# Per-step bonus and value copies of a linear-attention front end moved to other engines, with new due dates, in a fused attention, feed-forward and mixture-of-experts kernel

## The chip, the cores and the metric

The kernel runs on one core of one Trainium2 chip. The metric is the device time of one launch in microseconds, the median of several runs. The profiler's span is the time from the first to the last instruction of one profiled execution.

## What is computed

Three parts follow one another. The attention is a linear recurrence with a bonus for the present token (B = 4, H = 8 heads, S = 768, D = 48):

```
for t in range(S):
    kt, vt, rt = (k[:, :, t], v[:, :, t], r[:, :, t])
    cur = np.einsum('bhd,bhe->bhde', u[None] * kt, vt)
    y[:, :, t] = np.einsum('bhd,bhde->bhe', rt, state + cur)
    state = w[None, :, :, None] * state + np.einsum('bhd,bhe->bhde', kt, vt)
```

Its result, 3072 tokens of 384 numbers, goes through a feed-forward network `softplus(x @ w_in) @ w_out` with 2048 inner columns, and that result through eight experts. Tokens are assigned greedily by `x @ w_gate`, each expert takes 384 tokens, and its part is `relu(x @ w1[e]) @ w2[e]`.

The bonus of a token is `v * sum_d(r * k * u)`, one sum per head.

## The kernel before

The attention is done in 24 steps of 128 rows: 64 tokens of each of two batch entries. Three steps make a block of 384 tokens, and the feed-forward network works on eight such blocks. Step n loads k, r and v (`load_step`, lines 360 to 375, two DMAs of 96 KB each, in pieces of 48 numbers) into double buffers KN, RN, VN. It loads v once more in another layout into X, one of three tiles that also hold the recurrent state. In `attention` (line 444), VectorE multiplies k and r by tables of powers of w (ks and rs, lines 453 and 454), TensorE transposes both (lines 466 and 470), and the products of r and k over 64 tokens (line 491) are masked on VectorE (line 499). `fresh` (line 520) and `state` (lines 525 to 537) carry the state to the next X. The bonus is four VectorE operations, lines 541 to 544: r times k, times u (a tile ut with u on all partitions), a reduce over d, and v times the sums. TensorE then multiplies the masked products and the transposed r with X (line 553), and VectorE adds the bonus (line 558, tile xf).

For the first block the result is transposed on TensorE (line 566) and copied to the input of the feed-forward network. Steps 3 to 5, the second block, are transposed there too and split into two halves of 16 bit (lines 578 and 579). From step 6 on, the halves are made first (tile xhl, lines 583 to 585) and turned by a DMA transpose (`turn`, line 569).

Block 0 of the network runs in f32 (first layer at line 673, second at line 785). The later blocks run in three f16 products (lines 678 and 788 to 790). Weights arrive as pairs of 32-bit words, which VectorE puts together with three bit operations (lines 599 to 603) out of four raw buffers ("third<-moe_w_in", "third<-moe_w_out"); 16 such loads make the first layer. While it prepares the second layer, TensorE also transposes w_out (line 633) and multiplies it with the gate (line 637).

All of it up to the last expert is listed as items with an engine or a choice of engines, an assumed duration, dependencies and a due date. `lay_out` (line 148) is a planner that runs at build time. It lets time pass on assumed clocks of all engines and one for DMA, and always issues the ready item of earliest due date on the engine that is free first. The order so found is fixed; each engine then works through its own list and waits on semaphores. The due date of an attention step is `due_att(n)`. A transfer has an assumed `size` in ns of the DMA clock. Where the planner leaves a gap on TensorE it puts in fillers (`keep_warm`, line 143): matmuls on a tile of zeros, into a bank that nobody reads.

Of the kernel before, what the change touches and what calls it, by code (L numbers as in the profile page):

```python
# [21 lines left out]
def tile_kernel(ctx, tc, r, k, v, w, u, w_in, w_out, w_gate, w1, w2, out):  # L22
# [10 lines left out]
    HP = H // 2  # L33
# [216 lines left out]

    T0 = 15500.0
    LEN0 = 43500.0
# [20 lines left out]

    AHEAD = 7500.0

    TURNED, TURN = 6, 1500.0
    HALFL = 4000.0
    HALFL2 = -4000.0
    NLAT = 6
    LATL = 400.0  # L280
    OUTLATE = 5000.0
    RAWL = 17600.0
    BITL = 14000.0
    SPLITL = -3900.0
    WOUTL = 6100.0
    ATT0 = 2600.0
    LOADL = 1600.0

# [18 lines left out]
    XF = several(work, 2, [128, H * D], FT, "xf")  # L307
    XHL = several(work, 2, [128, 2 * DM], HF, "xhl")
    XT2 = several(ffn1p, 2, [128, 2 * KC, BT], HF, "xt")
# [50 lines left out]
    def load_step(n):  # L360
        GROUP[0] = "att"
        b0, s0 = step_tok(n)
        i = n % 2
        due = due_att(n) - LOADL
        for key, src, store in (("kn", k, KN), ("rn", r, RN), ("vn", v, VN)):
            for b in range(2):
                op("sp", 650.0, lambda b=b, src=src, store=store: SP.dma_start(
                    store[i][b * 64:(b + 1) * 64], src[b0 + b, :, s0:s0 + C, :].rearrange("h s d -> s h d")),
                    w=[(key, i, b)], due=due, size=546.0)
        for q in range(2):  # L370
            src = bass.AP(tensor=v.tensor, offset=v.offset + ((b0 * H + q) * S + s0) * D,
                          ap=[[D, C], [2 * S * D, 2 * HP], [1, D]])
            op("sp", 650.0, lambda q=q, src=src: SP.dma_start(
                X[n % 3][(1 - q) * 64:(2 - q) * 64, q].rearrange("p b a d -> p (b a) d"), src),
                w=[("xv", n % 3, q)], due=due + 3.0, size=546.0)

# [13 lines left out]
    op("sp", 1300.0, lambda: [SP.dma_start(wt[q * 64:q * 64 + D], w.rearrange("(p q) d -> q d p", q=2)[q])  # L390
                              for q in range(2)], w=["wt"], due=-1e9, size=168.0)
    op("sp", 450.0, lambda: SP.dma_start(
        ut, bass.AP(tensor=u.tensor, offset=u.offset, ap=[[0, 128], [1, H * D]])), w=["ut"], due=-500.0, size=546.0)
    op("sp", 450.0, lambda: SP.dma_start(gate, w_gate.rearrange("(k p) e -> p k e", p=128)),
# [17 lines left out]
    def powers():  # L412
# [5 lines left out]
        for i in range(6):  # L418
# [3 lines left out]
            DVE.tensor_mul(pw[:, 1, :, C - 2 * m:C - m], pw[:, 1, :, C - m:C], f)  # L422

    op("dve", 3200.0, powers, r=["wt"], w=["pw", ("ar", 1, 0)], due=-1e8)

# [18 lines left out]
    def attention(n):  # L444
# [62 lines left out]
        if n % PC < PC - 1:  # L507
# [27 lines left out]
            for q in range(2):  # L535
                rows = slice(q * 64, (q + 1) * 64)
                op({"act": 413.0, "dve": 470.0}, 0.0, lambda eng, rows=rows, q=q: copied(eng, X[y][rows, q], wx[rows].rearrange("p a b d -> p b a d")),
                   r=[("wx", 0), ("wx", 1)], w=[("st", y, q)], due=due + 3)


        product(rk, RN[i], KN[i], rnk + knk, ["rk"], due + 3)
        product(rk, rk, ut.rearrange("p (h d) -> p h d", h=H), ["ut"], ["rk"], due + 3)
        op("dve", 470.0, lambda: DVE.tensor_reduce(sd, rk, axis=AX.X, op=OP.add), r=["rk"], w=[("sd", i)], due=due + 3)
        product(sv, VN[i], sd[:, :, None].to_broadcast([128, H, D]), vnk + [("sd", i)], [("sv", i)], due + 3)

# [30 lines left out]
        if n < TURNED:  # L576
            op("pe", 321.0, tx, r=[("xf", i), "ident"], w=[(a, g, t) for a in ("xh", "xl", "x2")], due=due + 5, bank=b6)
            op(FROM_PSUM, 0.0, lambda eng: scaled(eng, hi, b6.view(KC, 128), 64.0), w=[("xh", g, t)], due=due + 5, bank=b6)
            op("dve", 470.0, lambda: DVE.scalar_tensor_tensor(lo, b6.view(KC, 128), 64.0, hi, op0=OP.mult, op1=OP.subtract),
               r=[("xh", g, t)], w=[("xl", g, t)], due=due + 5, bank=b6)  # L580
        else:
            xh, xl = XHL[i][:, :DM], XHL[i][:, DM:]
            op(FROM_SBUF, 0.0, lambda eng: scaled(eng, xh, xf, 64.0), r=[("xf", i)], w=[("xhl", i, 0)], due=due + 5)
            op("dve", 470.0, lambda: DVE.scalar_tensor_tensor(xl, xf, 64.0, xh, op0=OP.mult, op1=OP.subtract),
               r=[("xf", i), ("xhl", i, 0)], w=[("xhl", i, 1)], due=due + 5)
            op("sp", 700.0, turn, r=[("xhl", i, 0), ("xhl", i, 1)], w=[("xh", g, t), ("xl", g, t), ("x2", g, t)], due=due + 5, size=TURN)
# [6 lines left out]
    def from_double(src, t, key, due):  # L593
        c = WN[0]
        WN[0] += 1
        raw = RAW[c % 4]
        op("sp", 450.0, lambda: src(raw), w=[("raw", c % 4)], due=due - RAWL, size=1092.0)
        hi, lo = [raw[..., i] if len(t.shape) == 2 else raw[..., i].rearrange("p (k f) -> p k f", k=KC) for i in (1, 0)]
# [22 lines left out]
    def prep_wout(f):  # L621
# [18 lines left out]
        op(FROM_PSUM, 0.0, lambda eng: copied(eng, wT, b1.view(KC, 128)), w=[wt], due=due, bank=b1)  # L640
        op("pe", 330.0, mm, r=[wt, "gate"], due=due, bank=b2)
        op("act", 58.0, lambda: ACT.copy(t[:, DM:], b2.view(E)), w=[("wg", f + 1)], due=due, bank=b2)
# [741 lines left out]
    for p in range(E):  # L1384
# [7 lines left out]
        experts(p)  # L1392
    total = lay_out(items, lambda it: (it.prio, it.n), {}, True)
    s_ps.close()
# [24 lines left out]
```

## Time and profile before

| | us |
|---|---|
| median of 3 runs | 778.96 (777.51 to 786.61) |
| profiled execution, its own time | 775.64 |
| its span | 773.9 |
| TensorE busy (with fillers) | 749.8, 97% |
| VectorE busy | 624.9, 81% |
| ScalarE busy | 404.1, 52% |
| DMA queue q1, share of 16 engines | 38.3% |
| TensorE's share of the chain that ended last | 67% |

Busy time of TensorE counts matmuls from issue to a modelled end, fillers among them, so a busy TensorE may still be waiting for work. Idle time of an engine matters only where another waits for it.

### The profile page before, as it was taken

To read this page: it belongs to the slowest core of one execution; us is meant where nothing else is said; L and a number is where in the kernel's file an instruction comes from. 1 tells how busy PE (TensorE), PEld (TensorE's weight loads), DVE (VectorE), ACT (ScalarE), POOL (GpSimd) and SP (SyncE) were. 2 spreads that over 40 slices of the span, in tenths; PEclk is the share of its full clock that TensorE was granted. 3 is DMA by queue.
4 is the path that set the end of the run, shared out by engine and by line. 5 is a ranking of instruction groups with operands and counts; after the bars stand their busy time and mean duration, and the time that the engine had idled before them with its cause. 6 is when DMAs were issued, how large, how long until landed. Compare 5 with 4: busy or idle time off the path is not lost.

```text
span 773.9 us, 18327 instructions
## 1 busy us (share of the span) xinstructions
PE 749.8 (97%) x7202; PEld 493.0 (64%) x7202; DVE 624.9 (81%) x1711; ACT 404.1 (52%) x808; POOL 81.2 (10%) x109
## 2 busy tenths in 40 slices
PE   7999999999999999999999999999999999998996
PEld 6865677666566666667676666666666665655663
DVE  7898998999998787788999977887789879877420
ACT  2165533799766666567889911211145424436731
POOL 1000000000000000000001000000232131317731
PEclk9999999999999999999999999999999999999999
DMA  7887764412343233333110003441385664837700
GB/s 137 172 183 191 211 171 77 83 22 62 69 91 66 56 68 62 62 67 71 36 22 11 2 12 94 118 121 50 97 208 165 174 175 143 211 108 191 216 31 30
DMA packets 170901, 80.04 MB, mean 103 GB/s; under 512 B 136512, under 2 KB 166464, under 8 KB 170816
## 3 DMA queue, kind: packets, MB, share of 16 engines
q1 hardware_dynamic: 167744, 69.44, 38.3%
q0 software_dynamic: 3072, 9.44, 4.0%
q8 instruction: 56, 0.92, 0.5%
q14 instruction: 29, 0.24, 0.1%
HBM read 61.55 MB, written 9.63 MB: 92 GB/s over the span
## 4 chain that ended last, share of the span: by engine, by line
PE 67%; DVE 18%; issue 4%; ACT 4%; DMA 4%; SPq 1%; POOL 1%; POOLq 0%; ACTq 0%; DVEq 0%
PE bank L678 14%; PE bank L1292 7%; PE bank L788 7%; PE bank L789 6%; PE bank L790 6%; PE bank L785 3%; PE bank L1310 3%; PE bank L1312 3%; PE bank L1311 3%; PE bank L553 2%; PE bank L673 2%; DVE ar L499 2%; DVE gf L691 2%; PE bank L1036 2%; DMA mraw<-moe_w 1%
## 5 line engine op out<-in xcount | busy, mean ns | idle before, releaser
L678 PEld LDWEIGHTS <-wi 128*128 128x128 f16 x1008 | 97.3, 98 | 65.2 <-issue 2.0
L678 PE MATMUL bank<-xt,wi 128*128 128x384 f16 x672 | 127.6, 326 | 0.0
L684 ACT ACTIVATE ta<-bank 128x384 f32<-128x384 f32 x128 | 61.5, 482 | 43.3 <-PE bank L678 30.2
L789 PE MATMUL bank<-wo,g 128*128 128x384 f16 (+1 forms) x240 | 78.4, 327 | 0.9 <-DVE wo L649 0.7
L788 PE MATMUL bank<-wo,g 128*128 128x384 f16 (+1 forms) x240 | 78.5, 327 | 0.0
L790 PE MATMUL bank<-wo,g 128*128 128x384 f16 (+1 forms) x240 | 78.5, 327 | 0.0
L691 DVE SCALAR_TENSOR_TENSOR gf<-bank,ta 128x384 f32<-128x384 f32 x112 | 61.8, 553 | 17.2 <-ACT ta L686 16.0
L678 PE MATMUL bank<-xs,wi 128*128 128x384 f16 x336 | 72.9, 326 | 0.0
L1292 PE MATMUL bank<-g,w1h 128*128 128x384 f16 x384 | 72.9, 326 | 0.0
L685 ACT ACTIVATE ta<-ta 128x384 f32<-128x384 f32 x128 | 66.5, 522 | 2.9
L686 ACT ACTIVATE ta<-ta 128x384 f32<-128x384 f32 x128 | 66.2, 519 | 2.5
L1312 PE MATMUL bank<-w2h,g 128*128 128x384 f16 x192 | 62.6, 326 | 0.0
L1310 PE MATMUL bank<-w2h,g 128*128 128x384 f16 x192 | 62.6, 326 | 0.0
L1311 PE MATMUL bank<-w2l,g 128*128 128x384 f16 x192 | 62.5, 326 | 0.0
L1296 ACT ACTIVATE g<-bank 128x384 f16<-128x384 f32 x64 | 30.7, 489 | 40.4 <-PE bank L1292 24.7
L1292 PEld LDWEIGHTS <-w1h 128*128 128x128 f16 x384 | 35.8, 98 | 22.6 <-issue 0.4
L1299 DVE SCALAR_TENSOR_TENSOR g<-bank,g 128x384 f16<-128x384 f32 x64 | 34.1, 548 | 19.4 <-ACT g L1296 19.3
L698 DVE SCALAR_TENSOR_TENSOR g<-gf,g 128x384 f16<-128x384 f32 x80 | 44.0, 553 | 3.1 <-ACT g L345 1.8
L499 DVE TENSOR_TENSOR ar<-bank,mask 64x256 f32<-64x256 f32 x96 | 40.5, 422 | 4.6 <-PE bank L491 2.3
L345 ACT ACTIVATE x2o<-bank 128x384 f16<-128x384 f32 x19 | 9.3, 490 | 65.3 <-PE bank L790 39.2
L1205 POOL DMA_INDIRECT third<-x2d,idx x24 | 25.8, 1074 | 155.7 <-DVE db L1009 130.0
L1292 PE MATMUL bank<-g,w1l 128*128 128x384 f16 x192 | 41.7, 326 | 0.0
(227 smaller groups left out, 1533.3 us busy)
## 6 DMA issues: line engine op xcount, KB each, us to landing
mraw<-moe_w SPq DMA_DIRECT2D x64, 384.0 KB, 4.0
third<-moe_w_in SPq DMA_DIRECT2D x16, 384.0 KB, 5.0
third<-moe_w_out SPq DMA_DIRECT2D x16, 384.0 KB, 3.5
kn<-k SPq DMA_DIRECT2D x48, 96.0 KB, 3.1
rn<-r SPq DMA_DIRECT2D x48, 96.0 KB, 3.1
vn<-v SPq DMA_DIRECT2D x48, 96.0 KB, 3.0
X<-v SPq DMA_DIRECT2D x48, 96.0 KB, 3.1
x2d<-x2o SPq DMA_DIRECT2D x48, 96.0 KB, 2.2
```

What stands on the lines that cost most here:

```text
L678: PE.matmul(ph, WF[:, f, a, kk, :], x[:, kk, :], start=(i == 0), stop=(i == 3 * KC - 1))
L684: op("act", 371.0, lambda: ACT.activation(ta, bank.view(BT), AF.Abs), w=[("ta", c)], due=due, bank=bank)
L685: op("act", 413.0, lambda: ACT.activation(ta, ta, AF.Exp, scale=-1.0), w=[("ta", c)], due=due)
L686: op("act", 413.0, lambda: ACT.activation(ta, ta, AF.Ln, bias=1.0), w=[("ta", c)], due=due)
L691: op("dve", 470.0, lambda: DVE.scalar_tensor_tensor(gf, bank.view(BT), 0.0, ta, op0=OP.max, op1=OP.add), r=[("ta", c)], w=[("gf", c)], due ...
L788: PE.matmul(p, gh[:, f, ts], WU[:, f, 0, :no], start=(f == 0), stop=False)
L789: PE.matmul(p, gh[:, f, ts], WU[:, f, 1, :no], start=False, stop=False)
L790: PE.matmul(p, gl[:, f, ts], WU[:, f, 0, :no], start=False, stop=(f == FC - 1))
L1292: PE.matmul(ph, a[:, kk, fs], XH[p][:, x0 + kk, :], start=(i == 0), stop=(i == 3 * KC - 1))
L1310: PE.matmul(po, h1h[:, f, js], w2h[:, fz, :], start=(f == 0), stop=False)
L1311: PE.matmul(po, h1h[:, f, js], w2l[:, fz, :], start=False, stop=False)
L1312: PE.matmul(po, h1l[:, f, js], w2h[:, fz, :], start=False, stop=(f == FB - 1))
```

## The change

The first six steps get the bonus on TensorE. The transposed r (in its PSUM bank) and the transposed k, both with their powers of w, which leave one factor w in the product of a token with itself, are multiplied on VectorE into rkT. rkT lies in the buffers of xhl. Four f32 matmuls per step (`sums`), with rkT as the weight and a table uw of two columns (u times w of one head each), give the sums in PSUM, and VectorE multiplies v by them from there. The ut tile is needed only from step 6 on and is loaded later; u comes a second time, transposed, as uq. For the same steps X gets v by four copies from VN on ScalarE or VectorE, as the planner chooses, and the two DMAs are left out. TURNED goes from 6 to 3, so steps 3 to 5 are turned by DMA. Due dates and several assumed costs are new, the planner's clocks of SP and VectorE start at 1000 and 900 ns, and so every engine's order is new.

```diff
-    T0 = 15500.0
+    T0 = 16250.0
...
-    AHEAD = 7500.0
-
-    TURNED, TURN = 6, 1500.0
-    HALFL = 4000.0
-    HALFL2 = -4000.0
+    AHEAD = 10500.0
+
+    TURNED, TURN = 3, 1500.0
+    SUMMED = 6
+    COPIED = 6
+    HALFL = 9000.0
+    HALFL2 = -1500.0
...
-    OUTLATE = 5000.0
+    OUTLATE = 8750.0
...
-    BITL = 14000.0
+    BITL = 16000.0
...
-    ATT0 = 2600.0
-    LOADL = 1600.0
+    ATT0 = 850.0
+    LOADL = 2400.0
...
-    XHL = several(work, 2, [128, 2 * DM], HF, "xhl")
+    XHL2 = work.tile([128, 2, 2 * DM], HF, name="xhl")
+    XHL = [XHL2[:, i] for i in range(2)]
...
-                    w=[(key, i, b)], due=due, size=546.0)
+                    w=[(key, i, b)], due=due, size=640.0)
+        if n < COPIED:
+            for q in range(2):
+                for b in range(2):
+                    op({"act": 260.0, "dve": 180.0}, 0.0, lambda eng, q=q, b=b: copied(
+                        eng, X[n % 3][(1 - q) * 64:(2 - q) * 64, q, b],
+                        VN[i][b * 64:(b + 1) * 64].rearrange("p (a q) d -> p a q d", q=2)[:, :, q, :]),
+                        r=[("vn", i, b)], w=[("xv", n % 3, q)], due=due_att(n) + 2.5)
+            return
...
+    op("sp", 1300.0, lambda: [SP.dma_start(uq[q * 64:q * 64 + D], u.rearrange("(p q) d -> q d p", q=2)[q])
+                              for q in range(2)], w=["uq"], due=-1000.0, size=168.0)
     op("sp", 450.0, lambda: SP.dma_start(
-        ut, bass.AP(tensor=u.tensor, offset=u.offset, ap=[[0, 128], [1, H * D]])), w=["ut"], due=-500.0, size=546.0)
+        ut, bass.AP(tensor=u.tensor, offset=u.offset, ap=[[0, 128], [1, H * D]])), w=["ut"], due=due_att(3), size=1200.0)
...
+    uw = const.tile([128, HP, 2], FT, name="uw")
+    uq = const.tile([128, HP], FT, name="uq")
+    rkT = XHL2.rearrange("p a m -> p (a m)").bitcast(FT)[:, :HP * 128].rearrange("p (a t) -> p a t", a=HP)
+
+    def factors():
+        DVE.memset(uw, 0.0)
+        for q in range(2):
+            DVE.tensor_mul(uw[q * 64:q * 64 + D, :, q], uq[q * 64:q * 64 + D], wt[q * 64:q * 64 + D])
+
+    op("dve", 300.0, factors, r=["wt", "uq"], w=["uw"], due=2.5)
...
+        if n < SUMMED:
+            op("dve", 602.0, lambda: DVE.tensor_tensor(rkT, b2.view(HP, 128), kT, op=OP.mult), r=[("kT", i)], w=["rkT"] + [("xhl", a, b) for a in range(2) for b in range(2)],
+               due=due + 3, bank=b2)
+
+            def sums():
+                for pr in range(HP):
+                    PE.matmul(b7.view(H)[:, 2 * pr:2 * pr + 2], rkT[:, pr, :], uw[:, pr, :], start=True, stop=True)
+
+            b7 = Bank("att")
+            op("pe", 900.0, sums, r=["rkT", "uw"], w=[("sd", i)], due=due + 3, bank=b7)
+            op("dve", 470.0, lambda: DVE.tensor_tensor(sv, VN[i], b7.view(H)[:, :, None].to_broadcast([128, H, D]), op=OP.mult),
+               r=vnk, w=[("sv", i)], due=due + 3, bank=b7)
+        else:
+            bonus()
...
-        op("sp", 450.0, lambda: src(raw), w=[("raw", c % 4)], due=due - RAWL, size=1092.0)
+        op("sp", 450.0, lambda: src(raw), w=[("raw", c % 4)], due=due - RAWL, size=1900.0)
...
-        op("pe", 330.0, mm, r=[wt, "gate"], due=due, bank=b2)
+        op("pe", 670.0, mm, r=[wt, "gate"], due=due, bank=b2)
...
-    total = lay_out(items, lambda it: (it.prio, it.n), {}, True)
+    total = lay_out(items, lambda it: (it.prio, it.n), {"sp": 1000.0, "dve": 900.0}, True)
```

`bonus()` holds the four operations of lines 541 to 544. The order of the loads on SP at the very start, before (kn, rn, vn with numbers 93, 91, 95 are the buffers of even steps, 94, 92, 96 those of odd ones):

```order
L390 DMA wt<-w 48x4x1 x2
L607 DMA third<-moe_w_in 128x3x256
L367 DMA kn_93<-k 64x8x48 x2
L367 DMA rn_91<-r 64x8x48 x2
L367 DMA vn_95<-v 64x8x48 x2
L373 DMA X_97<-v 64x8x48 x2
L392 DMA ut<-u 128x384
L607 DMA third<-moe_w_in 128x3x256
L367 DMA kn_94<-k 64x8x48 x2
```

and now:

```order
L401 DMA wt<-w 48x4x1 x2
L370 DMA kn_93<-k 64x8x48 x2
L370 DMA rn_91<-r 64x8x48 x2
L370 DMA vn_95<-v 64x8x48 x2
L370 DMA kn_94<-k 64x8x48 x2
L370 DMA rn_92<-r 64x8x48 x2
L370 DMA vn_96<-v 64x8x48 x2
L647 DMA third<-moe_w_in 128x3x256
L403 DMA uq<-u 48x4x1 x2
```

The loads of the second step stand in fifth to seventh place, ahead of the first weight third; the X loads and ut are gone from this stretch.

VectorE in the third step (number 2, the even buffers), up to its result xf_114, before:

```order
L599 TENSOR_SCALAR wi<-third 128x384
L340 TENSOR_TENSOR rk_104<-rk_104,ut 128x384
L353 COPY ar_111<-bank_85 64x8x64
L527 TENSOR_TENSOR wx_113<-bank_86,wx_113 128x4x48
L527 TENSOR_TENSOR wx_113<-bank_81,wx_113 128x4x48
L543 TENSOR_REDUCE sd_105<-rk_104 128x8
L499 TENSOR_TENSOR ar_111<-bank_80,mask 64x4x64 x2
L499 TENSOR_TENSOR ar_111<-bank_82,mask 64x4x64 x2
L340 TENSOR_TENSOR wx_113<-wx_113,sq 128x384
L340 TENSOR_TENSOR sv_107<-vn_95,sd_105 128x384
L353 COPY X_97<-wx_113 64x384
L558 TENSOR_TENSOR xf_114<-bank_83,sv_107 128x384
```

and now, from the copy into ar_111 on:

```order
L356 COPY ar_111<-bank_85 64x8x64
L572 TENSOR_TENSOR xhl<-bank_85,kT_109 128x512
L641 SCALAR_TENSOR_TENSOR wi<-third,wi 128x384
L356 COPY X_99<-vn_95 64x192
L523 TENSOR_TENSOR ar_111<-bank_80,mask 64x4x64 x2
L356 COPY X_99<-vn_95 64x192
L523 TENSOR_TENSOR ar_111<-bank_81,mask 64x4x64 x2
L551 TENSOR_TENSOR wx_113<-bank_86,wx_113 128x4x48
L551 TENSOR_TENSOR wx_113<-bank_84,wx_113 128x4x48
L581 TENSOR_TENSOR sv_107<-vn_95,bank_83 128x384
L343 TENSOR_TENSOR wx_113<-wx_113,sq 128x384
L598 TENSOR_TENSOR xf_114<-bank_82,sv_107 128x384
```

The product with ut (line 340 into rk) and the reduce are replaced by one product into xhl's buffer (rkT, line 572), v is multiplied by a PSUM bank (line 581), and two of the value copies into X_99 stand between the masks.

TensorE around the sixteenth and last chunk of block 0's first layer, before (lines 466 and 470 belong to step 5, lines 633 and 637 prepare the second layer, line 785 is the second layer):

```order
L637 MATMUL bank_86<-gate,third 128x8 x3
L637 MATMUL bank_81<-gate,third 128x8 x3
L466 MATMUL bank_85<-identf,ks_103 128x128 x4
L673 MATMUL bank_86<-xt_118,wi 128x384 x3
L470 MATMUL bank_81<-identf,rs_101 128x128 x4
L633 MATMUL bank_85<-identf,wo 128x128 x3
L785 MATMUL bank_83<-wo,g_128 128x392 x2
```

and now (line 713 is the chunk, line 593 is step 6's product with X, line 577 the sums of step 5; lines 673 and 143 are the first preparation of the second layer and fillers):

```order
L593 MATMUL bank_82<-X_97,ar_111 64x48 x16
L577 MATMUL bank_84<-uw,xhl 128x2 x4
L713 MATMUL bank_81<-xt_117,wi 128x384 x3
L673 MATMUL bank_83<-identf,wo 128x128 x3
L143 LDWEIGHTS still
L143 MATMUL bank_87<-still 128x128
```

Steps 3 to 6 have now been through their product with X ahead of that chunk, where before it was steps 3 and 4, with step 5 begun; the preparation of the second layer starts behind it instead of ahead.

## Rows read from the trace of the kernel before

**Rows 1.** Windows: busy us (x instructions) by engine, then granted clock, DMA share, GB/s

```profile
0.00:39.00 39.00, 32.73 (x588) 29.13 (x588) 31.81 (x88) 8.82 (x15) 2.53 (x12) 0.96 0.76 154
39.00:86.00 47.00, 44.75 (x355) 28.87 (x356) 43.97 (x104) 26.65 (x56) 0.00 (x0) 1.00 0.78 193
86.00:142.00 56.00, 56.00 (x698) 40.91 (x697) 51.05 (x119) 22.92 (x57) 0.00 (x0) 1.00 0.60 138
142.00:774.00 632.00, 616.26 (x5565) 394.04 (x5563) 498.09 (x1404) 345.72 (x682) 78.72 (x97) 1.00 0.37 91
```

**Rows 2.** Groups by line, 0 to 40 us: the fillers; busy us, mean ns

```profile
L143 PE MATMUL bank<-still 128*128 128x128 bf16 x258 | 19.2, 233 | 1.0 <-DVE wt L389 1.0
```

**Rows 3.** Timeline, 0 to 38 us: start us, us, engine, line; in brackets the wait

```profile
16.59 0.56 DVE L340 TENSOR_TENSOR ks<-kn,pwn 128x384 f32<-128x384 f32 x1 [1.26 <-DMA kn<-k]
...
17.29 0.94 PE L466 MATMUL bank<-identf,ks 128*128 128x128 f32 x4 [1.51 <-DVE ks L340]
...
37.27 0.56 DVE L558 TENSOR_TENSOR xf<-bank,sv 128x384 f32<-128x384 f32 x1
...
37.88 0.55 PE L566 MATMUL bank<-identf,xf 128*128 128x128 f32 x3
```

**Rows 4.** Timeline of TensorE, 39 to 83 us

```profile
39.00 4.14 PE L673 MATMUL bank<-xt,wi 128*128 128x384 f32 x12
...
49.56 1.14 PE L553 MATMUL bank<-X,ar 128*64 128x48 f32 x32
...
52.67 0.49 PE L566 MATMUL bank<-identf,xf 128*128 128x128 f32 x3
...
62.46 0.66 PE L466 MATMUL bank<-identf,ks 128*128 128x128 f32 x4 [1.56 <-DVE ks L340]
...
81.36 1.50 PE L637 MATMUL bank<-gate,third 128*128 128x8 f32 x12
...
82.72 0.63 PE L466 MATMUL bank<-identf,ks 128*128 128x128 f32 x4
```

**Rows 5.** Window on VectorE, from the first ks to the third result

```profile
9.17:37.83 28.66, 23.08 (x53) 0.94 0.83 170
```

**Rows 6.** Groups of VectorE, 9.17 to 37.83 us: busy us, mean ns, idle before

```profile
L499 DVE TENSOR_TENSOR ar<-bank,mask 64x256 f32<-64x256 f32 x12 | 5.1, 422 | 0.4
...
L353 DVE COPY ar<-bank 64x512 f32<-64x512 f32 x3 | 2.1, 694 | 0.9 <-ACT ar L351 0.9
...
L340 DVE TENSOR_TENSOR rk<-rk,ut 128x384 f32<-128x384 f32 x3 | 1.7, 552 | 1.8 <-DMA ut<-u 1.8
...
L543 DVE TENSOR_REDUCE sd<-rk 128x8 f32<-128x384 f32 x3 | 1.6, 549 | 0.0
...
L527 DVE TENSOR_TENSOR wx<-bank,wx 128x192 f32<-128x192 f32 x4 | 1.2, 352 | 0.7 <-PE bank L520 0.7
...
L340 DVE TENSOR_TENSOR rk<-rn,kn 128x384 f32<-128x384 f32 x2 | 1.1, 548 | 0.0
...
L353 DVE COPY X<-wx 64x384 f32<-64x384 f32 x3 | 1.1, 356 | 0.1
```

**Rows 7.** Timeline of SP's issues, 6 to 10 us

```profile
6.60 1.31 SPq L373 DMA_DIRECT2D X<-v  x2
...
7.96 0.62 SPq L392 DMA_DIRECT2D ut<-u  x1
...
9.10 1.29 SPq L367 DMA_DIRECT2D kn<-k  x2
```

**Rows 8.** Timeline of VectorE: the late third, and the last first-layer weight

```profile
59.70 0.36 DVE L599 TENSOR_SCALAR wi<-third 128x384 int32<-128x384 int32 x1 [2.38 <-DMA third<-moe_w_in]
...
80.54 0.55 DVE L603 SCALAR_TENSOR_TENSOR wi<-third,wi 128x384 int32<-128x384 int32 x1
```

**Rows 9.** Windows of 1 us: busy us, TensorE's granted clock after POOL

```profile
16.00:17.00 1.00, 0.00 (x0) 0.00 (x0) 0.41 (x1) 0.00 (x0) 0.00 (x0) 1.00 0.36 64
18.00:19.00 1.00, 1.00 (x12) 0.97 (x10) 0.91 (x4) 0.59 (x1) 0.00 (x0) 0.50 1.12 184
```

More of the change, by code (lines that the diff above doesn't have):

```diff
@@ L374, in load_step @@
                 X[n % 3][(1 - q) * 64:(2 - q) * 64, q].rearrange("p b a d -> p (b a) d"), src),
-                w=[("xv", n % 3, q)], due=due + 3.0, size=546.0)
+                w=[("xv", n % 3, q)], due=due + 3.0, size=640.0)
     wt = const.tile([128, HP], FT, name="wt")
@@ L538, in attention, with bonus @@
                    r=[("wx", 0), ("wx", 1)], w=[("st", y, q)], due=due + 3)
[L541 to L544, printed above, removed]
+        def bonus():
+            product(rk, RN[i], KN[i], rnk + knk, ["rk"], due + 3)
+            product(rk, rk, ut.rearrange("p (h d) -> p h d", h=H), ["ut"], ["rk"], due + 3)
+            op("dve", 470.0, lambda: DVE.tensor_reduce(sd, rk, axis=AX.X, op=OP.add), r=["rk"], w=[("sd", i)], due=due + 3)
+            product(sv, VN[i], sd[:, :, None].to_broadcast([128, H, D]), vnk + [("sd", i)], [("sv", i)], due + 3)
+        if n < SUMMED:
[10 more added lines that the diff above has]
+            bonus()
         b5, b6 = Bank("att"), Bank("att")
@@ L582, in attention @@
             xh, xl = XHL[i][:, :DM], XHL[i][:, DM:]
-            op(FROM_SBUF, 0.0, lambda eng: scaled(eng, xh, xf, 64.0), r=[("xf", i)], w=[("xhl", i, 0)], due=due + 5)
+            op(FROM_SBUF, 0.0, lambda eng: scaled(eng, xh, xf, 64.0), r=[("xf", i)], w=[("xhl", i, 0), "rkT"], due=due + 5)
             op("dve", 470.0, lambda: DVE.scalar_tensor_tensor(xl, xf, 64.0, xh, op0=OP.mult, op1=OP.subtract),
```

## The prediction

> **What bounds the kernel now.** I read the stretches first. From 86 us to 142 us TensorE is busy 56.00 of 56.00 us and after that 616 of 632, so nearly all of the program is a queue of matmuls; what can be had lies ahead of 86 us. Before 39 us TensorE looks busy too (32.73 us), but the groups of the first 40 us show 258 fillers, matmuls on a zero tile that only keep the engine active, with 19.2 us of it [rows 1, 2]. They run where TensorE would wait. So I read the timeline of the first 39 us for what it waits for: the first matmul of the first feed-forward layer (line 673) starts at 39.00, right behind the ScalarE copy of the third step's transposed result, whose addition on VectorE (line 558) starts at 37.27 [rows 3, 4]. Three attention steps must be through before it, and they are a chain on VectorE: from the first ks product at 9.17 to the end of that addition at 37.83 VectorE works 23.08 of 28.66 us [rows 5]. The largest waits in it are two transfers: ut (1.8 us ahead of the product at line 542, as the group shows) and kn of the second step, 1.26 us ahead of 16.59 [rows 3, 6]. That kn is issued only at 9.10, because SP has put a weight third, the X copy of v and ut ahead of it, at 0.65 us an issue [rows 7].
>
> From 39 to 86 us TensorE (44.75 of 47) and VectorE (43.97 of 47) are both near full [rows 1]. TensorE's longest wait there, 1.56 us at 62.46, is for a ks product that stood behind a weight third that landed late (VectorE 2.38 us idle before 59.70) [rows 4, 8].
>
> **The change part by part.** *The way to the first layer.* In the new order on SP, kn, rn and vn of both first steps are the first twelve loads, and X and ut no longer stand between them; at the same 0.65 us an issue kn of the second step is issued at about 6 to 7.3 us instead of 9.10 to 10.4, with one weight third and the X pair less in the queue. Its ks product can start at about 11 instead of 16.59, and ut is not needed by the first six steps. I take both waits as gone: -3.1 us.
>
> VectorE's own list over these three steps: leaving are three products with ut (1.7 us), three reduces (1.6), two of the three r·k products (1.1; the first stood before 9.17) [rows 6]; the halving at line 347 (0.35, as the like operation at 59.70) and two of three state copies into X (2 x 0.36) go to ScalarE, which is busy 8.8 us of the first 39, or stand after the addition now. That is 5.5 us. Coming are three products of the transposed r and k (128x512 from PSUM). No row has this shape; between the 0.55 of a 128x384 operation and the 0.69 of the 64x512 PSUM copy I take 0.69, whose free size is the same: 2.1. Further the table uw (a fill and two products of 48x4; 0.4, hardly more than one such copy), three value copies left on VectorE (64x192; under the 0.36 of 64x384, I take 0.25: 0.75) and two more weight-preparing instructions (0.35 and 0.5) [rows 6, 8]. Sum 4.1, so the list is 1.35 us shorter.
>
> What is added in waits: the first value copy stands ahead of ks(0) on VectorE and, on ScalarE, two of them stand between the two copies of the power table; all wait for vn(0), which SP issues by about 6 us as its third pair. With ks(0) at 9.3 instead of 9.17 and rs(0) about 0.5 later than now, that hides behind the second ks. Behind the table uw on VectorE stand a weight third and the second step's state; uq, needed by it, is issued around 11 us and could take as long as kn did (issued by 10.4, used at 16.59), up to 1 us late. The sums on TensorE (four matmuls, two passes each) delay the next step's transpose on an engine full of fillers. So 28.66 - 3.1 - 1.35 = 24.2 us from 9.3, the addition ends at 33.5, and the first layer starts 1.17 us behind it as now (37.83 to 39.00): 34.7. **Term 1: -4.3 us.** If a part of the other 2.5 us idle goes too and the products take 0.55: -6.2; if uw comes late and the new hand-overs cost 1.5: -1.8.
>
> *TensorE's own work after that.* The sums of steps 3 to 5 lie in the full stretch. The nearest row is the gate product, 128x8 in f32 on a 128x128 weight: 12 records advance TensorE by 1.36 us (81.36 to 82.72), 0.113 each [rows 4]. Eight records a step are 0.92, three steps 2.8; bounds 1.6 (a narrower moving operand at 60% of it) and 3.2. Turning the results of the second block by DMA removes three transposes; the one at 52.67 takes 0.49 us with its latency, of which I take 0.35 as TensorE's own [rows 4]: -1.0. **Term 2: +1.8** (+0.1 to +2.2). For these steps ScalarE reads SBUF instead of PSUM and the transfer lands long before block 1 begins; its cover is the whole first layer. On SP a turn stands behind its step's VectorE work with two weight thirds behind it, but four third buffers are already issued ahead, so I cost it at nothing; without that cover it would cost what the late third at 59.70 cost.
>
> *The first layer, 39 to 86 us.* With X gone from the queue the 2.38 us wait of VectorE for a third, and with it TensorE's 1.56 us, should go. Against this the new due dates pull 1.5 attention steps ahead of the last first-layer chunk, and VectorE has to serve them. One step with the new sum is about 6.9 us there (ks, rs, state product, result addition and value product 0.5 to 0.55 each, masks 1.7, the two copies 0.69 and 0.36, states 0.7, the new product 0.69) [rows 3, 6], so 10.3 more; the two common steps save 1.5; weight preparation of the second layer moves behind (2.4), the split of the turned results and its copy drop 0.8; five more activation sums and half a preparation come (2.8): +8.4. The last first-layer weight, ready at 81.0 now [rows 8], would be ready at 81.0 - 4.3 + 8.4 - 2.4 = 82.7 and its chunk through at about 85, where it ends at 85.1 today. At that point TensorE will have done two more steps (six groups of small matmuls each, from 0.5 to the 1.1 of line 553 at 49.56: 3.2), less a begun one (0.9) and less second-layer preparation (2.2, by the 1.50 of its longest group): 3.3 us more useful work. So this path gives -3.5 in all, and I set **term 3: -1.0** (-2.7, that wait and as much again in small ones; +3, if VectorE is late again).
>
> **Sum:** -4.3 + 1.8 - 1.0 = -3.5 us against the profiled execution's 775.64 (its span 773.9 and 1.7 around it): 772.1. The runs' median, 778.96, lies 3.3 above that execution; a median of the changed kernel should stand alike: 775.4, a ratio of 0.995.
>
> **The clock.** With fillers taken away TensorE could fall to the lower clock. Now it has no work from 16 to 17 us, and from 18 to 19 the granted clock is 0.50, which is 1.2 of 2.4 GHz; the transposes at 17.29 take 0.94 us instead of the 0.66 they take at 62.46 [rows 3, 4, 9]. The Trainium skill (TensorE: Matmul & The Clock Gate, section "The HAM clock gate") says the low clock is the state to which an idle array falls back and activity is what releases it, and the trace agrees. By that rule the new order, with 188 fillers ahead of the first layer for 258, would pay once more if one of its gaps is as long as the one before 17.29; the sum itself keeps the clock as it is, since the gap that caused the fall (kn) goes.
>
> **The rivals.**
> *A, more than the sum.* VectorE, relieved by 0.75 us a step, keeps up, the late third and the small waits of 39 to 86 us all go, and the first layer starts at 33: -6.2 + 1.0 - 2 = -7, 772. For it: the DMA relief, twelve transfers of 96 KB less. Against: VectorE has more to do before the sixteenth chunk.
> *B, slower.* VectorE becomes the bound of the first layer. The 1.5 steps pulled ahead put 10.3 us on it in a stretch where it is already busy 43.97 of 47; if it waits there as much as today (3 us) and the hand-overs to TensorE and ScalarE cost 4 more, the last weight comes at 90, TensorE ends the layer at 92 with 3.3 us more done: 92 - 85.1 - 3.3 = +3.6, median 782.6. It decides from about 86 us for the last weight on. For it: both engines near full in one stretch; against: the count above, which has it at 82.7.
> *C, the change does not reach the end.* The start is earlier but the sums on TensorE and filler gaps behind the first layer eat it: -1.8 + 2.2 - 0.4 = 0, 779.
>
> **How the numbers follow.** Forecast (772.5 to 778) 0.50; A 0.22; C 0.15; B 0.13. The forecast's own bounds are -1.8 + 2.2 and -6.2 + 0.1 - 2.7 on the terms; the range 766 to 783 takes A's far end (-9.5 with the two runs' scatter of 3) and B. 2% is 15.6 us, about what a measurement of this kernel can tell from no change; only a start that gets nearly half of the fillers' time and the stalls back at once (763) would be faster by that, 0.04, and B would have to be four times as bad, 0.03; within 0.93.
>
> **What would show it.** Right: first matmul of the first layer at 34 to 36; second ks at about 11; no ut wait; no half clock before 25; the sums about 0.9 us a step; last first-layer weight at 82 to 84; TensorE full from 90 on with the same tail. Wrong: the first layer later than 37 (then uq, vn or the sums are in the chain, term 1), the last weight after 86 (B), a sum of over 1.2 us, or a changed stretch behind 142 us, which I took as it is.

## The result, and the profile after

The changed kernel takes 773.17 us (median of 20 runs, 770.23 to 775.0), the kernel before 780.16 in 20 runs beside it (775.66 to 786.61): a ratio of 0.9904, 95% interval 0.9885 to 0.9924. It is 1% faster, and the interval excludes 1. The forecast was 775.4 and 0.995: the sign and the range held, and the gain was about twice what was worked out. The profiled execution of the changed kernel took 770.23, with a span of 768.4 (773.9 before): 5.5 us less, where the sum said 3.5. The record has the mean granted clock of every run: 0.996 on average in these 20 runs, and 0.992 in the 82 runs of the kernel before that stand beside the experiments below. 0.004 of 775 us is 3.1 us, so by estimate some three of the seven us between the medians are less time at the low clock.

Windows of the changed kernel, with the columns of [rows 1]; the cuts at 33.40 (where the first layer starts), 86 and 142 us:

```profile
0.00:33.40 33.40, 30.68 (x541) 27.42 (x541) 29.04 (x84) 12.25 (x26) 2.53 (x12) 1.00 0.75 152
33.40:86.00 52.60, 51.17 (x565) 34.77 (x564) 50.89 (x118) 35.92 (x77) 0.00 (x0) 1.00 0.81 182
86.00:142.00 56.00, 55.37 (x513) 38.10 (x513) 54.06 (x124) 21.86 (x55) 0.00 (x0) 1.00 0.72 151
142.00:767.00 625.00, 613.01 (x5565) 392.48 (x5564) 486.87 (x1388) 337.47 (x669) 78.33 (x97) 1.00 0.36 90
```

The stretch ahead of the first layer is 5.6 us shorter than the 39.00 of [rows 1]. In the second stretch TensorE idles 1.43 us (2.25 before) and VectorE 1.71 (3.03 before): both are fuller than they were.

The timeline of the changed kernel: SP's issue of kn of the second step, the first three ks products, the table uw, the third step's addition, and the first layer ([rows 3, 4, 7] before):

```profile
6.12 1.31 SPq L370 DMA_DIRECT2D kn<-k  x2
8.55 0.56 DVE L343 TENSOR_TENSOR ks<-kn,pwn 128x384 f32<-128x384 f32 x1
10.13 0.55 DVE L343 TENSOR_TENSOR ks<-kn,pwn 128x384 f32<-128x384 f32 x1
...
15.93 0.07 DVE L443 MEMSET uw<- 128x8 f32 x1
16.03 0.35 DVE L445 TENSOR_TENSOR uw<-uq,wt 48x4 f32<-48x4 f32 x2
...
23.59 0.55 DVE L343 TENSOR_TENSOR ks<-kn,pwn 128x384 f32<-128x384 f32 x1
...
31.69 0.55 DVE L598 TENSOR_TENSOR xf<-bank,sv 128x384 f32<-128x384 f32 x1
32.30 0.55 PE L606 MATMUL bank<-identf,xf 128*128 128x128 f32 x3
33.41 4.14 PE L713 MATMUL bank<-xt,wi 128*128 128x384 f32 x12
```

kn is issued 3 us earlier than in [rows 7] and the second ks comes at 10.13 for 16.59. No bracket stands behind the two products with uq at 16.03, so VectorE does not wait for uq here.

The groups of the changed kernel in its first 40 us (fillers, and the new operations with the ones beside them) and the one wait of VectorE between 33 and 86 us:

```profile
L143 PE MATMUL bank<-still 128*128 128x128 bf16 x189 | 15.0, 238 | 1.0 <-DVE wt L400 1.0
L354 ACT COPY X<-vn 64x192 f32<-64x192 f32 x13 | 4.5, 350 | 1.2 <-DMA vn<-v 1.0
L577 PE MATMUL bank<-uw,xhl 128*128 128x2 f32 x24 | 3.2, 254 | 0.2 <-DVE xhl L572 0.2
L572 DVE TENSOR_TENSOR xhl<-bank,kT 128x512 f32<-128x512 f32 x3 | 2.1, 689 | 0.0
L581 DVE TENSOR_TENSOR sv<-vn,bank 128x384 f32<-128x384 f32 x3 | 1.7, 552 | 0.0
L356 DVE COPY X<-vn 64x192 f32<-64x192 f32 x4 | 1.0, 256 | 0.1
```
```profile
DVE ar L356 <- ACT ar L354: 0.7, 1, 0.7
```

The 2.38 us wait for a weight third of [rows 8] is gone, and TensorE's wait for ks with it; TensorE's longest wait there is now 1.0 us. The new 128x512 product takes 0.69 us and the 64x192 copy 0.26, as taken (0.69 and 0.25).

Further on, TensorE and the last first-layer weight on VectorE ([rows 4, 8] before):

```profile
41.84 1.05 PE L577 MATMUL bank<-uw,xhl 128*128 128x2 f32 x8
42.75 0.57 PE L713 MATMUL bank<-xt,wi 128*128 128x384 f32 x1
...
78.80 0.56 DVE L643 SCALAR_TENSOR_TENSOR wi<-third,wi 128x384 int32<-128x384 int32 x1
...
82.29 2.18 PE L713 MATMUL bank<-xt,wi 128*128 128x384 f32 x6
```

Eight records of a step's sums advance TensorE by 42.75 - 41.84 = 0.91 us (0.92 taken). The last weight is ready at 79.4, where 82.7 was expected.

**An account for TensorE.** From the first matmul of the first layer on, TensorE is full, so I split its time up to the last matmul of the f16 first layers (446.3 us before, 440.8 after) into idle time, fillers and the rest, its own work. The window with all instructions and the one with the fillers alone, first of the kernel before, then of the changed one:

```profile
39.00:446.30 407.30, 402.79 (x4324) 266.73 (x4325) 362.54 (x864) 283.05 (x609) 2.95 (x11) 1.00 0.37 80
39.00:446.30 407.30, 11.50 (x60) 5.62 (x60) 1.00 0.37 80
```
```profile
33.40:440.80 407.40, 404.54 (x4349) 268.25 (x4349) 361.23 (x866) 283.33 (x615) 2.73 (x11) 1.00 0.39 81
33.40:440.80 407.40, 10.97 (x69) 6.03 (x68) 1.00 0.39 81
```

The first number behind the length is the busy time: idle is 407.30 - 402.79 = 4.51 before and 2.86 after, fillers 11.50 and 10.97, own work 391.3 and 393.6. So the end, that last matmul, moved by -5.6 (start) - 1.65 (idle) - 0.53 (fillers) + 2.3 (own work) = -5.5 us, and from there on both kernels take 327.6 us. The same split of every run (us, one profiled execution each; "low clock" is the part of the own work lost at a granted clock under 1, from windows of 1 us; "behind" is the rest of the span, from the end to the last instruction). The last column is an estimate over all runs that the ratio uses: from the time of each, (1 - mean granted clock) x span is taken off, and the median of what is left is set against that of the kernel before beside it:

| | start | idle | fillers | own work | low clock in it | end | behind | median | ratio and interval | less low clock |
|---|---|---|---|---|---|---|---|---|---|---|
| before | 39.0 | 4.5 | 11.5 | 391.3 | 0 | 446.3 | 327.6 | | 1 | 0 |
| after | 33.4 | 2.9 | 11.0 | 393.6 | 0 | 440.8 | 327.6 | 773.17 | 0.9904 [0.9885, 0.9924] |  |
| e12_after | 33.4 | 2.9 | 11.0 | 395.2 | 1.7 | 442.4 | 329.8 | 773.09 | 0.9923 [0.9895, 0.9952] | -4.1 |
| e1_dates | 40.8 | 2.7 | 10.2 | 393.4 | 0 | 447.1 | 330.9 | 779.38 | 1.0016 [0.9993, 1.0039] | +3.6 |
| e2_parts | 35.0 | 5.2 | 10.4 | 397.7 | 5.1 | 448.3 | 329.5 | 777.05 | 0.9971 [0.9939, 1.0002] | -1.4 |
| e7_warm | 36.7 | 6.1 | 11.5 | 391.5 | 0 | 445.8 | 329.5 | 777.47 | 0.9976 [0.9946, 1.0006] | -0.3 |
| e8_loads | 36.2 | 5.8 | 14.2 | 393.2 | 1.7 | 449.4 | 325.9 | 777.9 | 0.9985 [0.9959, 1.001] | +0.6 |
| e11_copies_old | 36.4 | 4.4 | 11.5 | 391.3 | 0 | 443.6 | 335.4 | 777.27 | 0.9969 [0.9937, 1.0002] | -1.0 |
| e3_nosums | 35.0 | 1.6 | 11.9 | 391.2 | 0 | 439.7 | 330.6 | 770.51 | 0.9858 [0.981, 0.9906] | -6.5 |
| e5_noturn | 33.4 | 1.5 | 8.8 | 394.6 | 0 | 438.2 | 328.7 | 769.59 | 0.9858 [0.9808, 0.9907] | -6.4 |
| e6_sums2 | 33.5 | 2.1 | 11.0 | 395.5 | 0 | 442.1 | 329.5 | 776.51 | 0.9938 [0.9904, 0.9971] | -2.7 |
| e4_nocopies | 35.2 | 3.2 | 18.6 | 392.9 | 0 | 450.0 | 330.3 | 781.49 | 1.0014 [0.9979, 1.0049] | +4.8 |
| e9_nocopies_free | 35.9 | 1.5 | 12.0 | 392.5 | 0 | 441.8 | 332.2 | 774.36 | 0.9916 [0.9879, 0.9954] | -3.3 |
| e10_copies | 35.0 | 2.4 | 15.3 | 392.1 | 0 | 444.8 | 328.6 | 776.66 | 0.9985 [0.9955, 1.0014] | 0.0 |

The ends lie nearly in the order of the ratios. e2_parts and e8_loads, which lost clock in their profiled execution, end later than their ratios would have it. The experiments are read by these columns, with three cautions.

First, the clock. The 82 runs of the kernel before lie between 773.41 us (mean clock 0.998) and 790.21 (0.986). A line through them falls by 8.7 us for each 0.01 of clock, near the 7.8 that 1% of the span is, and more than half of their variance goes with it. In its profiled execution the kernel before lost 1.7 us ahead of its first layer ([rows 9]), which the account holds in the start. With the low clock taken off both, the ends differ from that of the kernel before by -3.8 (after), -3.9 (e12_after), -1.4 (e2_parts), -1.0 (e11_copies_old), -2.5 (e6_sums2) and -6.4 (e5_noturn), close to the last column. The others agree with it within 1.6, but e8_loads, which is 2.5 off.

Second, behind the end the profiled executions spread from 325.9 to 335.4 us, and the account does not cover that part: the profiled execution of e11_copies_old ends its span 5.1 us later than that of the kernel before, although its end is 2.7 earlier.

Third, one execution differs from the next. Up to its fillers e7_warm is the kernel before, yet it is 1.0 us earlier there (below). So differences of under 1 us in a term are not firm.

### The profile page after: what moved, and what is told of

Read it like the earlier page. It is cut to its first block, busy times and chain, and to the rows that moved or that the text cites. A ratio compares the mean times of both kernels' runs of the same rounds, so it can differ in the third digit from the quotient of the medians.

```text
span 768.4 us, 18301 instructions
## 1 busy us (share of the span) xinstructions
PE 750.2 (98%) x7179; PEld 492.8 (64%) x7179; DVE 620.9 (81%) x1710; ACT 407.5 (53%) x824; POOL 80.9 (11%) x109
## 4 chain that ended last, share of the span: by engine, by line
PE 65%; DVE 15%; issue 9%; DMA 3%; ACT 3%; POOL 2%; SPq 1%; POOLq 0%; DVEq 0%
PE bank L718 18%; PE bank L828 7%; PE bank L830 7%; PE bank L829 7%; PE bank L1332 5%; PE bank L593 3%; PE bank L825 2%; PE bank L1350 2%; PE bank L1352 2%; PE bank L1351 2%; PE bank L1076 1%; POOL out L1360 1%; PE bank L515 1%; DVE ar L523 1%; PE bank L713 1%
```

## The experiments

The theory was that the first layer starts earlier, that this reaches the end, and that the sums cost TensorE their own time. Its main rival was that an early start is eaten by the first layer, so that other parts or the dates bring the gain. In e7_warm, e6_sums2 and e12_after the order of every engine stays; after each of the other edits the planner lays it out anew, so what such a run shows is the price of a move together with that of an order.

**Dates alone, moves alone.** e1_dates is the changed kernel with all three moves undone:

```diff
-    TURNED, TURN = 3, 1500.0
-    SUMMED = 6
-    COPIED = 6
+    TURNED, TURN = 6, 1500.0
+    SUMMED = 0
+    COPIED = 0
...
-        ut, ...), w=["ut"], due=due_att(3), size=1200.0)
+        ut, ...), w=["ut"], due=-500.0, size=546.0)
```

> The changed kernel with all its due dates, assumed costs and clock starts, but none of the three moves: bonus on VectorE, v for X by DMA, steps 3 to 5 turned on TensorE; ut is loaded early again. If the moves bring the time (start theory): the X loads and ut stand in SP's queue again, the first matmul of the first layer starts at 37 to 40 us, and the total is within 3 us of the kernel before (ratio 0.996 to 1.004). If the new due dates bring it by themselves: first layer at about 35, ratio 0.990 to 0.993.

Measured: 1.0016; the first layer starts at 40.8. The dates alone bring nothing; with the low clock taken off they cost 3.6 us, by estimate. (The load of uq and the table uw, of no use here, are still in, and VectorE waits 0.80 us for uq.)

e2_parts has the three moves with the dates, costs and clock starts of before (ut's own date and cost, which go with the sums, stay new):

```diff
-    T0 = 16250.0
+    T0 = 15500.0
...
-    AHEAD = 10500.0
+    AHEAD = 7500.0
...
-    total = lay_out(items, lambda it: (it.prio, it.n), {"sp": 1000.0, "dve": 900.0}, True)
+    total = lay_out(items, lambda it: (it.prio, it.n), {}, True)
```

> The three moves with the old due dates, assumed costs and clock starts. Start theory: X and ut are out of the queue, so kn of step 1 is issued at about 7.5 to 9 us in place of 9.1 to 10.4 (a weight third still stands ahead of it), the first layer starts at 35 to 36.5, total 3 to 4 us under the kernel before (ratio 0.995 to 0.996). If the due dates bring it all: ratio 0.999 to 1.001.

Measured: 0.9971, and an interval that holds 1. The start is 4.0 us earlier, but the layer lasts to 91. Windows of this kernel, and the chunk of six matmuls that lies in them:

```profile
82.00:84.00 2.00, 1.84 (x15) 1.75 (x15) 1.89 (x7) 1.59 (x4) 0.00 (x0) 0.87 0.42 166
84.00:86.00 2.00, 2.00 (x31) 1.74 (x31) 1.89 (x4) 0.91 (x2) 0.00 (x0) 0.50 0.03 8
...
92.00:94.00 2.00, 2.00 (x8) 1.58 (x7) 2.00 (x6) 1.85 (x5) 0.00 (x0) 0.57 0.96 165
```
```profile
87.77 4.19 PE L713 MATMUL bank<-xt,wi 128*128 128x384 f32 x6
```

The granted clock is 0.50 (1.2 of 2.4 GHz) from 84 to 93 us, and six matmuls take 4.19 us that take 2.18 in the changed kernel at 82.29. That is 5.1 of the 448.3; without it the end would lie 3.1 us ahead of that of the kernel before, by estimate. The other nine runs bear it out: the four with a mean clock of 0.990 to 0.992 take 777.4 to 779.7 us, the three with 0.997 or more take 771.9 to 773.3, where the two runs of the kernel before at 0.997 beside them take 774.2 and 776.3. So the moves alone are worth something, by estimate 1.4 us, and the clock hides it.

**The start alone.** e7_warm is the kernel before with 26 fillers ahead of the second step's ks transposes, where TensorE fell to half clock in [rows 9]:

```diff
         def tk():
+            for _ in range(26 if n == 1 else 0):
+                PE.matmul(banks[7][:, :128], still, still, start=True, stop=True)
             for pr in range(HP):
```

> The kernel before with 26 more filler matmuls ahead of the transposes of step 1's ks, where TensorE waits 1.5 us for that product; nothing else moves. If the clock matters: the granted clock stays at 1.00 from 15 to 21 us, the chain behind it gets 0.5 to 1 us shorter, the runs scatter less than those of the kernel before, ratio 0.997 to 0.999. If the clock at that place costs nothing on the way to the first layer: ratio 1.000, same scatter.

Measured: 0.9976, interval holding 1. The same two windows as [rows 9], then VectorE between them and the first layer, in the kernel before:

```profile
16.00:17.00 1.00, 1.00 (x17) 0.99 (x15) 0.94 (x3) 0.00 (x0) 0.00 (x0) 1.00 0.63 106
18.00:19.00 1.00, 1.00 (x51) 0.94 (x44) 1.00 (x2) 0.00 (x0) 0.00 (x0) 1.00 0.93 270
```
```profile
20.67 0.62 DVE L527 TENSOR_TENSOR wx<-bank,wx 128x192 f32<-128x192 f32 x2 [0.65 <-PE bank L520]
...
23.01 0.69 DVE L353 COPY ar<-bank 64x512 f32<-64x512 f32 x1 [0.62 <-ACT ar L351]
```

and in e7_warm, with the late third and TensorE's longest wait from 33 to 90 us (us in total, times, longest):

```profile
15.60 0.56 DVE L340 TENSOR_TENSOR ks<-kn,pwn 128x384 f32<-128x384 f32 x1 [0.83 <-DMA kn<-k]
...
19.06 0.62 DVE L529 TENSOR_TENSOR wx<-bank,wx 128x192 f32<-128x192 f32 x2
...
20.70 0.69 DVE L353 COPY ar<-bank 64x512 f32<-64x512 f32 x1
...
34.95 0.56 DVE L560 TENSOR_TENSOR xf<-bank,sv 128x384 f32<-128x384 f32 x1
...
58.75 0.36 DVE L601 TENSOR_SCALAR wi<-third 128x384 int32<-128x384 int32 x1 [3.74 <-DMA third<-moe_w_in]
```
```profile
PE bank L468 <- DVE ks L340: 2.9, 1, 2.9
```

The clock holds and the first layer starts 2.3 us earlier. Not all of that is the clock. The second ks is already 1.0 us earlier (15.60 for the 16.59 of [rows 3]), because ut and kn landed earlier in this execution; kn is issued at 9.1 us in both kernels, and the fillers run from 15.05 on. From that ks to the third step's addition it takes 19.35 us for 20.68, and the two waits of 0.65 and 0.62 are gone: the half clock cost about 1.3 us at the start, by one execution of each kernel.

But the late third is used only 0.95 us earlier than in [rows 8] (58.75 for 59.70), VectorE now waits 3.7 us for it and TensorE 2.9 (2.38 and 1.56 before, [rows 4, 8]), and the end moves by 0.5. Here the main rival is right: the first layer eats most of the earlier start, and the lower median goes with the higher clock (-0.3 us without it).

e8_loads is the kernel before with the loads of the second step put ahead of the X loads and ut:

```diff
-        due = due_att(n) - LOADL
+        due = due_att(n) - LOADL if n != 1 else -1598.0
...
-        ut, ...), w=["ut"], due=-500.0, size=546.0)
+        ut, ...), w=["ut"], due=-500.0 + 1500.0, size=546.0)
```

> The kernel before, with only step 1's loads of k, r and v moved ahead of the X loads, and ut behind the second weight third, in SP's queue; the planner orders all else anew. Start theory: the wait for kn (1.3 us) goes, the one for ut may move, second ks at 11 to 13 us in place of 16.6, first layer at 36.5 to 38, total 1 to 2.5 us under the kernel before (0.997 to 0.999). If the three moves of the bonus and copies are needed to shorten VectorE's chain: first layer at 38.5 to 39, ratio 1.000.

Measured: 0.9985. The start is 2.8 us earlier, but VectorE waits 5.6 us for one third, idle grows by 1.3, fillers by 2.7, and 1.7 us go to the low clock:

```profile
DVE wi L599 <- DMA third<-moe_w_in: 5.6, 1, 5.6
```

e11_copies_old is the kernel before with the value copies alone (e2_parts with SUMMED = 0, TURNED = 6 and ut loaded early again):

> The kernel before with the value copies alone, with the old dates, planner costs and clock starts. Theory that copies and dates are needed together: 0.995 to 1.000, span 773 to 776, the first layer starting 2 to 4 us earlier than 39 us and ending no earlier than 84. Rival, that the copies alone bring the gain: as the run of copies with new dates, 0.980 to 0.990, span 764 to 769.

Measured: 0.9969. The start is 2.6 us earlier, idle, fillers and own work are those of before, and the end moves by 2.7. With the X loads gone the early start does carry through: VectorE's wait for a third is down to 1.1 us here:

```profile
DVE wi L639 <- DMA third<-moe_w_in: 1.1, 1, 1.1
```

The ratio agrees (0.31% is 2.4 us), though the interval just holds 1. Part of this is the clock: the granted clock is 1.00 up to the first layer here, and with the low clock taken off both kernels 1.0 us is left.

**One move taken back.** e3_nosums has the bonus on VectorE again (and ut loaded early), e5_noturn the transposes of steps 3 to 5 on TensorE, e4_nocopies the X loads:

```diff
-    SUMMED = 6
+    SUMMED = 0
```


> The changed kernel with the bonus back on VectorE in the first six steps and ut loaded early; value copies, turns and dates as changed. If the bonus move carries part of the gain: VectorE's list to the first layer is about 2 to 2.5 us longer and ut may be waited for, first layer at 36 to 38, ratio to the kernel before 0.994 to 0.998. If loads and dates carry it alone: ratio 0.990, as the changed kernel.

```diff
-    TURNED, TURN = 3, 1500.0
+    TURNED, TURN = 6, 1500.0
```


> The changed kernel with steps 3 to 5 turned on TensorE again. If the turns are worth the 1.0 us taken for them: ratio about 0.992 for 0.990. If the late xhl turns cost time on SP: 0.988 or less.

```diff
-    COPIED = 6
+    COPIED = 0
```


> The changed kernel with v loaded into X by DMA in the first six steps. If the X loads out of SP's queue are what matters: step 1's ks at 13 or later, first layer at 36 to 38, weight thirds late in the first layer, ratio 0.996 to 1.000. If the bonus move carries it: first layer at 34 to 35, ratio 0.990 to 0.993.

Measured: 0.9858, 0.9858 and 1.0014. Without the sums, own work is 2.4 us less than in the changed kernel; without the turns it is 1.0 more: both terms were sized nearly right (2.8 and 1.0). Yet both kernels end earlier than the changed one, e5_noturn because fillers are 2.2 us and idle 1.4 us less, e3_nosums because idle is 1.3 less besides the sums, against a start 1.6 us later. The ratio of e3_nosums lies below both expectations (0.990 was the lower), though its interval reaches 0.9906. For e5_noturn the figure set for late turns on SP came out (0.988 or less), but the account shows fillers and idle of TensorE and no cost of the turns. Without the copies the gain is gone, but so much of that is fillers (+7.7 us) that the loads themselves are not yet charged.

e6_sums2 does the sums of steps 3 to 5 twice:

```diff
-                for pr in range(HP):
+                for pr in list(range(HP)) * (2 if n >= 3 else 1):
```


> The changed kernel with the four sums of steps 3, 4 and 5 done twice (the second writes the same values); the order of all else is kept. If TensorE's time there goes straight to the end, as term 2 says: 3 x 0.9 us more, ratio to the kernel before about 0.994 for 0.9904. If TensorE has slack there because VectorE bounds the first layer: under 1 us more, ratio 0.990 to 0.9915.

Measured: 0.9938. By the price own work should grow by 3 x 0.91 = 2.7 us. In the profiled execution it grows by 1.9, 0.7 of that falls into what was idle time, and the end moves by 1.3, half of the price. The ratio is 0.15% to 0.34% (1.2 to 2.7 us) above the two measurements of the changed kernel, with intervals that overlap. With the low clock taken off, it is 1.4 us above e12_after (-2.7 against -4.1), as the end has it. So about half of the price arrives at the end, by one profile and an estimate over the runs.

**What undoing the copies really cost.** In e9_nocopies_free the X loads are back, but the planner costs them at 1 ns of its DMA clock instead of 640, beside COPIED = 0. The line holds for the X loads of all 24 steps; twelve of them are new against the changed kernel (48 for 36), not the 24 that the expectation counts:

```diff
-                w=[("xv", n % 3, q)], due=due + 3.0, size=640.0)
+                w=[("xv", n % 3, q)], due=due + 3.0, size=1.0)
```


> The changed kernel with the value copies undone (values of the first six steps come by 24 more DMAs, as before), but with each of these DMAs costed at 1 ns in the planner's DMA clock instead of 640, so that the planner does not delay the steps and fill up: 30 fillers stand behind the first first-layer matmul and ahead of the second layer, 119 in the run that only undid the copies, 25 in the changed kernel. Theory that the DMAs themselves cost (SP's issue time and the weight thirds behind them): as without the copies, 1.001 of the kernel before, span 777 to 780, and TensorE waits in 40 to 90 us for thirds. Rival, that the loss without the copies was the planner's own fillers: 0.988 to 0.992, span 767 to 770, as the changed kernel.

Measured: 0.9916, as e12_after (0.9923), the changed kernel on the same chip:

> The changed kernel itself, beside the three others on the same chip: 0.987 to 0.993 by every theory. It is the yardstick for whether copies and dates alone beat it by more than 0.3%.

The windows of the fillers alone, of e4_nocopies and e9_nocopies_free:

```profile
35.20:450.00 414.80, 18.63 (x181) 12.73 (x181) 1.00 0.41 81
```
```profile
35.90:441.80 405.90, 11.98 (x77) 6.57 (x77) 1.00 0.42 83
```

The two kernels do the same work with the same DMAs. One number of the planner takes out 104 fillers, 6.65 us, and the end comes 8.2 us earlier. So the reading that the copies are the part that carries the gain falls: within the new dates, and with the planner's cost changed, they are worth nothing that these runs can measure, and e4_nocopies lost by its order.

e10_copies undoes sums and turns together (with ut loaded early) and leaves copies and dates:

> The changed kernel with the bonus back on VectorE in all steps and no DMA turns in steps 3 to 5: value copies and new dates alone. Undoing either one alone gave 0.986. Theory that each of the two moves costs TensorE or a wait its own 2 to 3 us: the sum of the two gains, 0.980 to 0.984, span 764 to 766. Rival, that both runs only removed the same wait and the rest is VectorE's time: 0.985 to 0.990, span 767 to 770, with fillers in the place of the sums (70 behind the first first-layer matmul and ahead of the second layer, 25 in the changed kernel).

Measured: 0.9985, outside both expectations. Two moves that can each be undone with nothing lost can't both be. The window of its fillers:

```profile
35.00:444.80 409.80, 15.26 (x130) 9.60 (x130) 1.00 0.37 79
```

Against e5_noturn, which has the sums, own work is 2.5 us less, but fillers are 6.5 more, idle 0.9 more and the start 1.6 later: +6.6 at the end. Against e3_nosums, which has the turns, own work is 0.9 more, fillers 3.4 more, idle 0.8 more: +5.1. With copies and dates alone the planner expects TensorE to wait and fills up. Whether TensorE would have waited there without fillers was not tried.

## Why the prediction was right, and where it was off

The direction was right for the reasons given: the first layer starts earlier, its sums cost TensorE what they were said to, and the stretch behind is as long as before. Without the 1.7 us of low clock at the start of the kernel before, the spans differ by 3.8 us by estimate, near the 3.5 of a sum that left the clock out; but its terms were each off by 0.5 to 1.3.

VectorE in the changed kernel from the first ks to the third result, with the columns of [rows 5]:

```profile
8.55:32.24 23.69, 21.61 (x51) 1.00 0.85 178
```

- **Term 1** (-4.3) measured -5.6. From the first ks to the end of the third addition VectorE takes 23.7 us, where 24.2 was worked out. Busy time fell by 1.5 (23.08 to 21.61; 1.35 was taken) and idle time by 3.5 (5.58 to 2.08; 3.1 was taken). The first ks was set at 9.3 and starts at 8.55. uq was in time, where up to 1 us late had been allowed for. The step that failed is that the sum keeps the clock as it is: in the kernel before the half clock cost about 1.3 us on this way beside the waits for kn and ut (e7_warm), and in the changed kernel the granted clock is 1.00 over the whole stretch. These three make 4.4 us of idle time, of which 3.5 went, so about 0.9 us of other idle time came. That the 3.1 for the waits came so near is luck.
- **Term 2** (+1.8) measured +2.3: sums 2.4 (against 2.8), transposes -1.0 (as said), and 0.9 left over. As much stands in e10_copies with the new dates (392.1), more in e1_dates (393.4), and none in e11_copies_old with the old ones (391.3). It seems to come with the dates; which work it is, is open.
- **Term 3** (-1.0) measured -2.2: idle -1.65, fillers -0.5. The late third went, as said, and VectorE was not late again. The last weight came 3.3 us before its time (79.4 for 82.7), 1.3 of it from the earlier start; the count of VectorE's work was too dear by the other 2.0.
- **Rivals.** A (start at 33, 772) came near: the result lies between forecast and A, in the profiled span as in the median, and a little nearer to A. B is refuted (last weight at 79.4; it needed 86). C did not happen here, but an early start that does not reach the end is what e7_warm and e8_loads had (by waits for a third, and in e8_loads fillers and clock, not by sums), so it deserved more than a sentence on fillers.
- **What would show it.** The second ks (10.13), the sums (0.91 us a step) and the clock came as said. The first layer (33.4 for 34 to 36) and the last weight (79.4 for 82 to 84) came earlier.
- **What the prediction did not see** is the planner. The prediction took -4.3 at the start as -4.3 at the end. The start reaches the end in e11_copies_old and not in e7_warm or e8_loads; what differs there is whether a third lands in time and how many fillers the order has. The gain belongs to no single move: sums, turns or X copies can each be undone (the last with the planner's cost changed) without loss, and dates alone or copies with dates alone bring nothing measurable. The dates with the moves bring more than the moves alone (4.1 against 1.4 us with the low clock taken off).

e5_noturn, the changed kernel without the DMA turns of the second block, had the lowest median in this study (769.59; four runs, 769.01 to 771.76; the changed kernel 770.23 to 775.0). It beats the kernel before; against the changed kernel the intervals overlap (0.9808 to 0.9907 and 0.9885 to 0.9924), so that it beats that one too is not settled.

## What to carry to other kernels

Where an engine is full from some point on, write its time as start, idle, fillers and own work, and compare kernels term by term: that told apart runs whose totals said little. Before charging a loss to an operation that was put back, change only what the planner believes of it; here an assumed cost was worth 8 us (e4_nocopies against e9_nocopies_free) and the operation about nothing. And look at the next late transfer before counting an earlier start: in e7_warm and e8_loads it did not move along, and the start was lost.

## What the runs showed of the hardware

The granted clock also falls to 0.50 where the rows show TensorE busy. e12_after has the changed kernel's own order; its windows of 1 us at 391, and the groups of TensorE in the 3.1 us ahead of them:

```profile
391.00:392.00 1.00, 1.00 (x33) 0.88 (x31) 0.97 (x5) 1.00 (x3) 0.00 (x0) 0.88 0.00 0
392.00:393.00 1.00, 1.00 (x5) 0.44 (x3) 0.93 (x6) 0.93 (x3) 0.00 (x0) 0.50 0.00 0
393.00:394.00 1.00, 1.00 (x4) 0.44 (x3) 1.00 (x4) 0.79 (x2) 0.00 (x0) 0.50 0.00 0
```
```profile
L755 PE MATMUL bank<-wo,third 128*128 128x16 f16 x48 | 2.6, 169 | 0.0
L756 PE MATMUL bank<-wo,third 128*128 128x8 f16 x47 | 2.6, 166 | 0.1
```

What the engine did before it fell is a row of matmuls 8 and 16 columns wide. In e2_parts, too, narrow ones stand ahead of the fall at 83 (eight of a step's sums, 128x2, and six gate products, 128x8, from 81.66 on). They don't suffice: the first profile of the changed kernel has the same row of matmuls at 389 to 392 at a clock of 1.00. In e8_loads the fall at 49 follows 3.3 us without work, behind the late third; the one of [rows 9] follows such a gap too.

So two executions of one kernel differ by 1.7 us at 440 us, and the falls behind that (one at 705 in e12_after) add 1.5 net: 3.2 of the 3.8 us between their spans of 768.4 and 772.2. Profiles, and medians too, are to be compared with the time at the low clock taken out.
